# mLSTM cell with mixture of depths: exponents by matrix product, output gates by tanh, state decay on GpSimd, and another order of the layers

## The chip, the cores and the metric

The kernel runs on one core of a Trainium2 chip. The metric is device time in microseconds, from start to end of one execution; the median of several executions counts. A core has a matrix engine (TensorE, "PE" in the profile, with its weight loads as "PEld"), a vector engine (VectorE, "DVE"), a scalar engine for activation functions (ScalarE, "ACT"), a general engine (GpSimd, "POOL"), and a queue engine (SyncE, "SP") which here only issues transfers. Sixteen DMA engines move data between the device memory and the on-chip SBUF; TensorE writes to PSUM, from where VectorE or ScalarE fetch the result.

## What is computed

There are two stages: an mLSTM cell over 4 batches, 8 heads, 768 positions and 40 elements a head, and a mixture of depths over the 4 x 768 tokens of 8 x 40 = 320 elements that it yields.

```python
for t in range(S):                                   # _attn_ref, per batch and head
    m_new  = np.maximum(f_gate[:, :, t] + m, i_gate[:, :, t])
    f_stab = np.exp(f_gate[:, :, t] + m - m_new)
    i_stab = np.exp(i_gate[:, :, t] - m_new)
    m = m_new
    C = f_stab * C + i_stab * einsum('bhd,bhe->bhde', vt, kt)
    n = f_stab * n + i_stab * kt
    h_tilde = einsum('bhde,bhe->bhd', C, qt)
    denom = np.maximum(np.abs(nq), 1.0)              # nq = n . q
    y[:, :, t] = sigmoid(o_gate[:, :, t]) * h_tilde / denom

scores = np.einsum('bsd,d->bs', x, w_gate)           # _moe_ref
out = x.copy()
for b in range(B):
    top_idx = np.argpartition(-scores[b], capacity)[:capacity]      # capacity 128
    xe = x[b, top_idx]
    ye = np.maximum(xe @ w1, 0.0) @ w2                               # 320 -> 1024 -> 320
    out[b, top_idx] = xe + sigmoid(scores[b, top_idx])[:, None] * ye
```

Both kernels compute the first stage in chunks of 128 positions: inside a chunk as a masked matrix of weighted products of keys and queries, between chunks by a state C that decays. There are 6 chunks in a batch and 24 in all.

## The kernel before

The gates are handled for all 32 rows (batch x head) at once. A running sum F of the forget gates and a running maximum Mg of a = i - F are made chunk by chunk. Mg is written to device memory (M_d), so that it can be read back spread over all 128 partitions; a comes as one column for each head.

```python
for c in range(NT):
    nc.vector.tensor_tensor_scan(out=F[:, c, :], ...)                     # L143
    nc.vector.tensor_tensor(out=a[:, c, :], in0=i_sb[:, c, :], in1=F[:, c, :], op=OP.subtract)
    nc.vector.tensor_tensor_scan(out=Mg[:, c, 0:L], ...)                  # L146
    ...
    nc.scalar.dma_start(out=M_d[c], in_=Mg[:, c, :])
    pc = ps_t.tile([128, 3, BH], FP, name="pc", tag="t")
    for j, row in enumerate((a, wk, r)):
        nc.tensor.transpose(pc[:, j, :], row[:, c, :], ident[0:BH, 0:BH]) # L157
    ...
```

Every chunk loads k, q, v and the spread Mb. The weights W = exp(a - M) are made by one activation for each head, with a as its bias; the mask is set beforehand.

```python
def load_chunk(b, c):
    ...
    nc.sync.dma_start(out=Mb, in_=_bcast(M_d[c][b * H:(b + 1) * H, :], 128))

def mlstm_chunk(b, c, qk, v1, Mb, C, so, x, sc):
    nc.gpsimd.affine_select(out=Mb[:, :, 0:L], ..., fill=BIG, ...)        # L177
    for h in range(H):
        nc.scalar.activation(out=W[:, h // 2, h % 2, :], in_=Mb[:, h, 0:L], func=AF.Exp,
                             bias=cols[c][:, 0, ...], scale=-1.0)         # L181
    # ... pt: transposes of k and q (L188), copied to qkT by ScalarE (L189)
    # ... pS = k q (L198), P = pS * W on VectorE (L200)
    # ... pI = C q (L207), num = pI * r (L210)
    # ... wv = v * wk on GpSimd (L215), pC = k wv (L221)
    for j in range(2):
        nc.vector.tensor_tensor(out=Cj, in0=Cj, op=OP.mult, in1=decay...) # L229
        nc.vector.tensor_tensor(out=Cj, in0=Cj, in1=pj, op=OP.add)        # L231
    # ... pH = P v (L236), num = num + pH (L240), den, rec (L243 to L246)
    nc.gpsimd.tensor_tensor(out=sor, in0=so[:, c], in1=rec..., op=OP.mult)         # L248
    nc.vector.tensor_tensor(out=x[:, c, :]..., in0=num[:, :, 0:D], in1=sor, ...)   # L249
    nc.vector.tensor_tensor_reduce(out=scr, in0=x[:, c, :], in1=wg, ..., accum_out=sc[:, c:c + 1])  # L252
    for dst in (x_d[b], out[b]):
        nc.gpsimd.dma_start(out=dst[c * L:(c + 1) * L, :], in_=x[:, c, :])         # L255
```

The output gates of a whole batch are loaded and put through a sigmoid in one piece. `compare` sets the scores of one chunk against those of all chunks so far (pb L262, sb L263, ge L265); `ranks` makes ranks of them (pcol L274, sel); `gather` finds the chosen rows (pidx) and fetches them by an indirect transfer from x_d (L301); `layer1` and `layer2` are the two layers (ph L331, py L342), after which ye is written to its rows in out by an indirect transfer (L345). The layers of a batch come in one piece, in the fifth chunk of the next batch; of the last two batches' layers, all come after the last chunk:

```python
            elif c == NT // 2 + 1 and b < B - 1:
                layer2(b - 1, layer1(b - 1, todo))
    compare(*steps[-1], *state[B - 1][1])
    before_last = layer1(B - 2, todo) if B > 1 else []
    sels = ranks(B - 1, *state[B - 1][1][2:])
    layer2(B - 2, before_last)
    layer2(B - 1, layer1(B - 1, gather(B - 1, sels)))
```

A framework around the kernel sets all waits by which tile is written and read by whom, and puts the instructions of each engine in an order of its own; pools of buffers decide when a tile may be written anew.

Of the kernel before, what the change touches and what calls it, by code (L numbers as in the profile page):

```python
# [9 lines left out]
FP = mybir.dt.float32  # L10
# [17 lines left out]
def kernel(  # L28
# [35 lines left out]
    NB = 4  # L64
    GE = [L * u * (u + 1) // 2 for u in range(NT + 1)]
    HALVES = [slice(0, 64), slice(64, 128)]
    AHEAD = 2

    assert S == NT * L and D < DP and H == 2 * NP and BH <= 128 and F_ == NFC * 128 and 0 < capacity < S <= 2048
# [14 lines left out]
    f_sb = gate.tile([BH, NT, L], FP, name="f_sb")  # L84
    i_sb = gate.tile([BH, NT, L], FP, name="i_sb")
    nc.sync.dma_start(out=f_sb, in_=f_gate.rearrange("b h (c p) -> (b h) c p", p=L))
    nc.sync.dma_start(out=i_sb, in_=i_gate.rearrange("b h (c p) -> (b h) c p", p=L))
# [3 lines left out]
    for n in range(NB):  # L91
        nc.gpsimd.memset(qk_t[n][:, :, :, D:DP], 0.0)
        nc.gpsimd.memset(v_t[n][:, :, D:DP], 1.0)

    def load_chunk(b, c):
        n = (b * NT + c) % NB
        t = slice(c * L, (c + 1) * L)
        for j, src in enumerate((k, q)):
            nc.sync.dma_start(out=qk_t[n][:, j, :, 0:D], in_=src[b, :, t, :].rearrange("h p d -> p h d"))  # L99
        nc.sync.dma_start(out=v_t[n][:, :, 0:D], in_=v[b, :, t, :].rearrange("h p d -> p h d"))  # L100
        Mb = work.tile([128, H, L + 1], FP, name="Mb", bufs=NB)
        nc.sync.dma_start(out=Mb, in_=_bcast(M_d[c][b * H:(b + 1) * H, :], 128))
        return qk_t[n], v_t[n], Mb

    ident = const.tile([128, 128], FP, name="ident")
    make_identity(nc, ident)
    iota_i = const.tile([128, capacity], I32, name="iota_i")
    nc.gpsimd.iota(iota_i, pattern=[[1, capacity]], channel_multiplier=0)
    iota_f = const.tile([128, capacity], FP, name="iota_f")
    nc.vector.tensor_copy(out=iota_f, in_=iota_i)  # L110

    token_i = const.tile([128, NT], I32, name="token_i")
    nc.gpsimd.iota(token_i, pattern=[[L, NT]], channel_multiplier=1)
    token = const.tile([128, NT], HF, name="token")
    nc.vector.tensor_copy(out=token, in_=token_i)
    later = const.tile([128, NT], FP, name="later")
    nc.vector.tensor_scalar(out=later, in0=token_i, scalar1=-1.0, scalar2=float(S - 1), op0=OP.mult, op1=OP.add)
    earlier = const.tile([128, NT * L], BF, name="earlier")
    nc.gpsimd.memset(earlier, 1.0)
    nc.gpsimd.affine_select(out=earlier[:, S - L:], in_=earlier[:, S - L:], compare_op=OP.is_gt, fill=0.0, base=0,  # L120
                            pattern=[[-1, L]], channel_multiplier=1)
    ones_b = const.tile([128, 1], BF, name="ones_b")
    nc.gpsimd.memset(ones_b, 1.0)
    xe_t = [const.tile([128, NDC * 128], FP, name=f"xe{n}") for n in range(2 * len(SLOTS))]
    n_xe = [0]
    for n in range(len(xe_t)):
        nc.gpsimd.memset(xe_t[n], 0.0)
    x_d = [dram.tile([S, DM], FP, name=f"x_d{b}") for b in range(B)]
    ones = const.tile([BH, L], FP, name="ones")
    nc.vector.memset(ones, 1.0)  # L130


    F = gate.tile([BH, NT, L], FP, name="F")
    a = gate.tile([BH, NT, L], FP, name="a")
    Mg = gate.tile([BH, NT, L + 1], FP, name="Mg")
    r = gate.tile([BH, NT, L], FP, name="r")
    wk = gate.tile([BH, NT, L], FP, name="wk")
    m = gate.tile([BH, NT + 1], FP, name="m")
    nM = gate.tile([BH, NT], FP, name="nM")
    nc.vector.memset(m[:, 0:1], -BIG)  # L140
    M_d, cols = [], []
    for c in range(NT):
        nc.vector.tensor_tensor_scan(out=F[:, c, :], data0=ones, data1=f_sb[:, c, :], initial=0.0,  # L143
                                     op0=OP.mult, op1=OP.add)
        nc.vector.tensor_tensor(out=a[:, c, :], in0=i_sb[:, c, :], in1=F[:, c, :], op=OP.subtract)
        nc.vector.tensor_tensor_scan(out=Mg[:, c, 0:L], data0=ones, data1=a[:, c, :], initial=m[:, c:c + 1],  # L146
                                     op0=OP.mult, op1=OP.max)
        nc.vector.tensor_tensor(out=m[:, c + 1:c + 2], in0=F[:, c, L - 1:L], in1=Mg[:, c, L - 1:L], op=OP.add)
        nc.vector.tensor_scalar(out=nM[:, c:c + 1], in0=Mg[:, c, L - 1:L], scalar1=-1.0, scalar2=None, op0=OP.mult)
        nc.scalar.activation(out=r[:, c, :], in_=Mg[:, c, 0:L], func=AF.Exp, bias=m[:, c:c + 1], scale=-1.0)  # L150
        nc.scalar.activation(out=wk[:, c, :], in_=a[:, c, :], func=AF.Exp, bias=nM[:, c:c + 1], scale=1.0)
        nc.vector.tensor_copy(out=Mg[:, c, L:L + 1], in_=r[:, c, L - 1:L])
        M_d.append(dram.tile([BH, L + 1], FP, name=f"M_d{c}"))
        nc.scalar.dma_start(out=M_d[c], in_=Mg[:, c, :])
        pc = ps_t.tile([128, 3, BH], FP, name="pc", tag="t")
        for j, row in enumerate((a, wk, r)):
            nc.tensor.transpose(pc[:, j, :], row[:, c, :], ident[0:BH, 0:BH])  # L157
# [275 lines left out]
```

## Time and profile before

| Quantity | Value |
|---|---|
| Time, median of three executions | 268.16 us (264.06 to 270.69) |
| Profiled execution: span | 261.3 us |
| Mean granted TensorE clock | 0.88 of full speed |
| Bytes moved | 41.07 MB, mean 157 GB/s |
| W, exponents: 192 activations | 61.2 us of ACT, 392 ns each |
| qkT, evictions: 48 copies of 128x512 | 26.9 us of ACT, 581 ns each |
| Table loads on ACT | 11 of 1283 ns |
| C, decay: 32 products of 40x164 | 11.9 us of DVE, 371 ns each |
| ph, first layer: 192 matmul instructions | 27.1 us of PE |
| py, second layer: 64 matmul instructions | 18.0 us of PE |

A line of instructions in the profile gives start, duration, engine, line of the kernel, operation, the tile written and the tiles read, and in brackets how long the engine had been idle before it and what ended that. A line of waits gives who waited for whom, the total in microseconds, the number of waits and the longest. A line of a queue gives packets, megabytes and the share of sixteen engines' span. A stretch gives its bounds and length, then busy time (and number of instructions) of PE, PEld, DVE, ACT and POOL, then the granted clock, the DMA share and GB/s. The DMA line has one digit, in tenths, for each fortieth of the span.

### The profile page before, as it was taken

What the parts mean: (1) busy time and instruction counts of PE and PEld (TensorE: products, weight loads), DVE (VectorE), ACT (ScalarE), POOL (GpSimd) and SP (SyncE); (2) the same over time, 40 slices, a digit from 0 to 9 for tenths busy, and PEclk for the clock granted to TensorE, in tenths of its full rate; (3) what the DMA queues carried; (4) which work ended last, traced back from release to release, by engine and by line L of the source; (5) the groups of instructions that cost most, each with busy time, mean ns of one, the idle gap of its engine ahead of it and who ended that gap; (6) DMA issues with size and microseconds to landing.
All of it is one profiled execution on the core that took longest, in us unless ns stands there. A gap on an engine that the chain in (4) does not pass through costs nothing.

```text
span 261.3 us, 6263 instructions
## 1 busy us (share of the span) xinstructions
PE 189.9 (73%) x2402; PEld 160.6 (61%) x2402; DVE 148.7 (57%) x443; ACT 120.1 (46%) x304; POOL 105.5 (40%) x155
## 2 busy tenths in 40 slices
PE   0498204875987968899799687998969862982980
PEld 0376103764966856887687576976859752961950
DVE  5813303687767998831779799347876985021000
ACT  2484049776568455760556578237633300000000
POOL 8435322635365455643643655443354222003001
PEclk9999855797799988799999979999995995798696
DMA  8979899999799899996599999717533121001000
GB/s 119 147 272 222 288 205 226 224 194 238 163 238 264 198 203 230 238 185 227 102 177 215 221 211 258 222 75 152 130 81 113 41 75 50 3 0 50 3 0 25
DMA packets 107085, 41.07 MB, mean 157 GB/s; under 512 B 101328, under 2 KB 101520, under 8 KB 107056
## 3 DMA queue, kind: packets, MB, share of 16 engines
q1 hardware_dynamic: 103392, 28.61, 55.8%
q0 software_dynamic: 3376, 11.96, 13.6%
q8 instruction: 19, 0.31, 0.5%
q10 hardware_dynamic: 288, 0.10, 0.2%
q14 instruction: 10, 0.08, 0.1%
HBM read 32.05 MB, written 8.62 MB: 156 GB/s over the span
## 4 chain that ended last, share of the span: by engine, by line
issue 23%; DMA 20%; DVE 19%; PE 12%; SPq 10%; POOL 10%; ACT 2%; POOLq 1%; ACTq 0%; DVEq 0%
DMA Mb<-M_d 10%; POOL sor L248 5%; SPq L350 5%; PE pH L236 3%; DVE P L200 3%; DVE x L249 3%; SPq L100 3%; DMA out_dram<-x 3%; PE ph L331 2%; DMA qk<-in_k_dram 2%; SPq L99 2%; DVE ge L265 2%; POOL Mb L177 2%; DMA so<-in_o_gate_dram 2%; DVE C L229 2%
## 5 line engine op out<-in xcount | busy, mean ns | idle before, releaser
L181 ACT ACTIVATE W<-Mb,cols 128x128 f32<-128x128 f32 x192 | 61.2, 392 | 22.8 <-POOL Mb L177 11.8
L236 PE MATMUL pH<-v,P 128*64 128x64 f32 x768 | 30.9, 232 | 24.9 <-DVE P L200 19.7
L236 PEld LDWEIGHTS pH<-v,P 128*64 128x64 f32 x768 | 26.5, 144 | 30.9 <-issue 15.4
L200 DVE TENSOR_TENSOR P<-pS,W 128x512 f32<-128x512 f32 x48 | 31.9, 680 | 17.0 <-ACT W L181 16.6
L177 POOL TENSOR_SCALAR_AFFINE_SELECT Mb<-Mb 128x1024 f32<-128x1024 f32 x24 | 26.9, 1121 | 35.8 <-DMA Mb<-M_d 35.0
L198 PE MATMUL pS<-qkT 64*128 64x128 f32 x384 | 35.6, 319 | 3.0 <-ACT qkT L189 3.0
L188 PE MATMUL pt<-ident,qk 128*128 128x128 f32 x192 | 35.2, 309 | 1.1 <-ACT qkT L189 0.8
L198 PEld LDWEIGHTS pS<-qkT 64*128 64x128 f32 x384 | 29.3, 216 | 7.9 <-ACT qkT L189 4.2
L248 POOL TENSOR_TENSOR sor<-so,rec 128x320 f32<-128x320 f32 x24 | 17.3, 722 | 40.8 <-DVE rec L246 31.7
L189 ACT COPY qkT<-pt 128x512 f32<-128x512 f32 x48 | 26.9, 581 | 14.3 <-PE pt L188 14.2
L331 PE MATMUL ph<-xeT,w 128*128 128x128 f32 x192 | 27.1, 311 | 3.0 <-DVE xeT L323 1.6
L331 PEld LDWEIGHTS ph<-xeT,w 128*128 128x128 f32 x192 | 26.3, 225 | 4.1 <-DVE xeT L323 2.2
L188 PEld LDWEIGHTS pt<-ident,qk 128*128 128x128 f32 x192 | 23.4, 154 | 4.1 <-ACT qkT L189 1.4
L207 PE MATMUL pI<-C,qkT 128*64 128x128 f32 x320 | 25.3, 307 | 0.0
L249 DVE TENSOR_TENSOR x<-num,sor 128x320 f32<-128x320 f32 x20 | 11.4, 570 | 18.9 <-POOL sor L248 18.9
L215 POOL TENSOR_TENSOR wv<-v,cols 128x328 f32<-128x328 f32 x20 | 15.1, 754 | 17.3 <-PE pC L221 6.5
L207 PEld LDWEIGHTS pI<-C,qkT 128*64 128x64 f32 x320 | 20.0, 154 | 2.9 <-issue 0.8
L265 DVE SCALAR_TENSOR_TENSOR ge<-sb,sc,earlier 128x128 bf16<-128x128 f32 (+5 forms) x24 | 19.9, 830 | 2.9 <-ACT sb L263 2.4
L255 POOL DMA_DIRECT2D x_d<-x x24 | 14.1, 590 | 17.7 <-DVE x L249 17.1
L262 PE MATMUL pb<-ident,sc 128*128 128x128 f32 x24 | 8.5, 356 | 15.8 <-DVE sc L252 15.8
L344 DVE SCALAR_TENSOR_TENSOR ye<-py,g,xe 128x320 f32<-128x320 f32 x4 | 2.2, 550 | 30.8 <-PE py L342 30.8
L263 ACT COPY sb<-pb 128x128 f32<-128x128 f32 x24 | 6.2, 260 | 28.5 <-PE pb L262 28.5
(84 smaller groups left out, 250.1 us busy)
## 6 DMA issues: line engine op xcount, KB each, us to landing
Mb<-M_d SPq DMA_DIRECT2D x24, 516.0 KB, 5.6
qk<-in_k_dram SPq DMA_DIRECT2D x24, 160.0 KB, 5.1
qk<-in_q_dram SPq DMA_DIRECT2D x24, 160.0 KB, 5.0
v<-in_v_dram SPq DMA_DIRECT2D x24, 160.0 KB, 4.5
so<-in_o_gate_dram SPq DMA_DIRECT2D x24, 160.0 KB, 4.6
x_d<-x POOLq DMA_DIRECT2D x24, 160.0 KB, 3.2
out_dram<-x POOLq DMA_DIRECT2D x24, 160.0 KB, 3.6
w<-in_moe_w_dram POOLq DMA_DIRECT2D x1, 1280.0 KB, 12.8
```

The source lines that it names most:

```text
L177: nc.gpsimd.affine_select(out=Mb[:, :, 0:L], in_=Mb[:, :, 0:L], compare_op=OP.is_ge, fill=BIG, base=0, pattern=[[0, H], [1, L]], channel_m ...
L181: nc.scalar.activation(out=W[:, h // 2, h % 2, :], in_=Mb[:, h, 0:L], func=AF.Exp, bias=cols[c][:, 0, b * H + h:b * H + h + 1], scale=-1.0)
L188: nc.tensor.transpose(pt[:, p, :], qk[:, j, 2 * p:2 * p + 2, :].rearrange("s a d -> s (a d)"), ident)
L189: nc.scalar.copy(out=qkT[:, j], in_=pt)
L198: nc.tensor.matmul(pS[j][:, p, :], qkT[e, 0, p, :], qkT[e, 1, p, :], start=True, stop=True)
L200: nc.vector.tensor_tensor(out=P[:, :, j, :], in0=pS[j], in1=W[:, :, j, :], op=OP.mult)
L207: nc.tensor.matmul(pI[t, 2 * p:2 * p + 2, :].rearrange("t a d -> t (a d)"), qkT[:, 1, p, t], C[:, p].rearrange("e a d -> e (a d)"), start= ...
L236: nc.tensor.matmul(pH[t, h, :], P[:, h // 2, h % 2, t], v1[:, h, :], start=True, stop=True)
L248: nc.gpsimd.tensor_tensor(out=sor, in0=so[:, c], in1=rec.unsqueeze(2).to_broadcast([128, H, D]), op=OP.mult)
L249: nc.vector.tensor_tensor(out=x[:, c, :].rearrange("p (h d) -> p h d", d=D), in0=num[:, :, 0:D], in1=sor, op=OP.mult)
L265: nc.vector.scalar_tensor_tensor(out=ge[:, GE[u]:GE[u + 1]], in0=sb.rearrange("p t l -> p (t l)")[:, 0:n], scalar=sc[:, u:u + 1], in1=earl ...
L331: nc.tensor.matmul(ph[:, f, :], w1[:, j, (f0 + f) * 128:(f0 + f + 1) * 128], xeT[:, j, :], start=(j == 0), stop=(j == NDC - 1))
```

## The change

The change has seven parts.

1. **Exponents by a product.** Instead of spreading Mg by a transfer through device memory, a - M is made by TensorE. M and a are each split into three bf16 numbers whose sum is the fp32 number, and placed (by a product with a table, `place`) in 32 rows for each group of four heads, beside rows of ones; a bf16 product over these 32 rows then gives a - M of four heads at once, 128x512, in PSUM. One exponent evicts it. The mask comes after that, on W. This removes M_d, Mb and the bias columns. The gates are loaded four times, into four groups of 32 partitions, since the placement reads the parts from there; the scans run over several chunks at once.
2. **Output gates by tanh.** sigmoid(x) = (1 + tanh(x/2)) / 2; tanh and 1 + ... are done on each chunk's gates, which are loaded with the chunk, and the factor 2 goes into the denominator.
3. **Decay on GpSimd.** There are three state buffers; GpSimd writes the decayed state into the next one and VectorE adds the new part.
4. **x stored once.** The gather reads from out instead of from x_d, and the indirect transfers name only the rows up to their own batch.
5. **Layers over three chunks.** First half of layer 1 in the fourth chunk, second half in the fifth, layer 2 in the sixth. For the third batch layer 1 so lies in the last batch.
6. **Ranking first in the tail.** The last batch's ranking and gather come ahead of the third batch's layer 2.
7. **Preparation one chunk ahead.** W, wv, the transposes and the tanh of chunk n + 1 (`prepare`) are written before the rest of chunk n; loads run three chunks ahead with five buffers instead of two with four.

```diff
-    NB = 4
+    NB = 5
-    AHEAD = 2
+    AHEAD = 3
...
+    def load_f_i(c0, c1):
+        for dst, src, eng in ((f_sb, f_gate, nc.sync), (i_sb, i_gate, nc.scalar)):
+            for g in G:
+                eng.dma_start(out=dst[g, c0:c1], in_=src.rearrange("b h (c p) -> (b h) c p", p=L)[:, c0:c1])
...
+    def split(x3, x, g):
+        nc.vector.tensor_copy(out=x3[:, g], in_=x[:, g])
+        nc.vector.tensor_tensor(out=rest[64:128, g], in0=x[64:128, g], in1=x3[64:128, g], op=OP.subtract)
+        nc.vector.tensor_copy(out=x3[64:128, g], in_=rest[64:128, g])
+        nc.vector.tensor_tensor(out=x3[96:128, g], in0=rest[96:128, g], in1=x3[96:128, g], op=OP.subtract)
+        nc.vector.memset(x3[0:BH, g], 1.0)
+
+    def operands(u, c):
+        pX = ps_m.tile([128, 2, L], FP, name="pO", tag="m")
+        for j, x3 in enumerate((M3, a3)):
+            nc.tensor.matmul(pX[:, j, :], place[j][u]..., x3[:, c, :], start=True, stop=True)
+        ...
+        nc.scalar.copy(out=a_o[u, c], in_=pX[:, 1, :])
+        nc.vector.tensor_tensor(out=M_o[u, c], in0=pX[:, 0, :].unsqueeze(1).to_broadcast([128, 4, L]), op=OP.mult,
+                                in1=which.unsqueeze(2).to_broadcast([128, 4, L]))
...
+    def prepare(b, c, qk, v1, so):
+        for h0 in range(0, H, 4):
+            rows_in = slice(64 * (b % 2) + 8 * h0, 64 * (b % 2) + 8 * h0 + 32)
+            pW = ps_t.tile([128, 4, L], FP, name="pW", tag="t")
+            nc.tensor.matmul(pW, a_o[b // 2, c][rows_in], M_o[b // 2, c][rows_in], start=True, stop=True)
+            nc.scalar.activation(out=W[:, h0:h0 + 4, :], in_=pW, func=AF.Exp)
+        nc.gpsimd.affine_select(out=W, in_=W, compare_op=OP.is_ge, fill=0.0, base=0, ...)
+        ...                                    # wv; transposes pt, copied to T
+        nc.scalar.activation(out=so, in_=so, func=AF.Tanh, scale=0.5)
+        nc.scalar.add(so, so, 1.0)
...
-        for h in range(H):
-            nc.scalar.activation(out=W[:, h // 2, h % 2, :], in_=Mb[:, h, 0:L], func=AF.Exp, ...)
...
+                nc.gpsimd.tensor_tensor(out=Cn[:, :, :, 0:D1], in0=C[:, :, :, 0:D1], op=OP.mult, ...)
-                    nc.vector.tensor_tensor(out=Cj, in0=Cj, op=OP.mult, in1=decay...)
...
-        for dst in (x_d[b], out[b]):
-            nc.gpsimd.dma_start(out=dst[c * L:(c + 1) * L, :], in_=x[:, c, :])
+        nc.gpsimd.dma_start(out=out[b, c * L:(c + 1) * L, :], in_=x[:, c, :])
...
+    def rows(b):
+        return out[0:b + 1].rearrange("b s d -> (b s) d")
...
+    load(0)
+    load_f_i(1, NT)
+    gates(0, 1)
+    prepared(0)
+    load(1)
+    gates(1, 3)                                # gates(3, NT) at the second chunk
...
-            elif c == NT // 2 + 1 and b < B - 1:
-                layer2(b - 1, layer1(b - 1, todo))
+            elif c == 3:
+                todo = enter(todo)
+                layer1(todo, 0)
+            elif c == 4:
+                layer1(todo, 1)
+            elif c == 5 and b < B - 1:
+                layer2(b - 1, todo)
     compare(*steps[-1], *state[B - 1][1])
-    before_last = layer1(B - 2, todo) if B > 1 else []
-    sels = ranks(B - 1, *state[B - 1][1][2:])
-    layer2(B - 2, before_last)
-    layer2(B - 1, layer1(B - 1, gather(B - 1, sels)))
+    picked = gather(B - 1, ranks(B - 1, *state[B - 1][1][2:]))
+    if B > 1:
+        layer2(B - 2, todo)
+    picked = enter(picked)
+    for half in range(2):
+        layer1(picked, half)
+    layer2(B - 1, picked)
```

Here the names of the pieces are new where the order asks for it: `gates(c0, c1)` does the scans, maxima, split and operands of the chunks c0 to c1 - 1, and `enter` gathers the gate value and the transposes of the chosen rows that `layer1` did before.

## The prediction

> **What bounds the kernel now.** I read the head of the page first, then the DMA line in 40 slices with the table of queues, then the stretches, the table of waits, and the timeline at both ends.
>
> ```profile
> span 261.3 us, 6263 instructions
> PE 189.9 (73%) x2402; PEld 160.6 (61%) x2402; DVE 148.7 (57%) x443; ACT 120.1 (46%) x304; POOL 105.5 (40%) x155
> DMA  8979899999799899996599999717533121001000
> q1 hardware_dynamic: 103392, 28.61, 55.8%
> q0 software_dynamic: 3376, 11.96, 13.6%
> ```
>
> No engine is full, but the transfers are near full until about 170 us. The loads (q1) carry 28.61 MB: 24 Mb broadcasts of 516 KB (12.7 MB) and 96 loads of 160 KB. Next the stretches; the columns are PE, PEld, DVE, ACT and POOL busy, the granted clock, the DMA share and GB/s:
>
> ```profile
> 30.00:40.00 10.00, 0.00 (x0) 0.00 (x0) 0.00 (x0) 3.73 (x3) 3.92 (x6) 0.56 1.04 198
> 40.00:75.00 35.00, 26.42 (x378) 22.66 (x380) 24.30 (x64) 26.35 (x73) 15.76 (x22) 0.78 1.04 211
> 110.00:145.00 35.00, 31.91 (x433) 26.71 (x432) 21.61 (x59) 17.67 (x51) 15.52 (x22) 1.00 0.83 186
> 180.00:218.00 38.00, 29.75 (x485) 25.39 (x483) 30.07 (x93) 14.02 (x40) 14.26 (x22) 0.88 0.33 90
> 0.00:218.00 218.00, 162.61 (x2240) 137.24 (x2240) 142.78 (x426) 117.28 (x298) 101.33 (x150) 0.90 0.83 184
> ```
>
> There are three regimes. Up to 75 us the transfers bind, with ten microseconds in which PE does nothing. From 110 us PE is the fullest engine (31.91 of 35). At the end of the body the DMA share is 0.33 and yet PE has 8 us idle of 38: there DVE (30.07) and its exchange with POOL set the pace. The waits name the two causes:
>
> ```profile
> POOL Mb L177 <- DMA Mb<-M_d: 35.0, 18, 4.9
> POOL sor L248 <- DVE rec L246: 31.7, 14, 4.3
> DVE x L249 <- POOL sor L248: 22.4, 24, 2.2
> ```
>
> The score instructions (scr, one for each chunk) serve as milestones: the first two and the last from the DVE timeline.
>
> ```profile
> 26.07 0.49 DVE L252 CUSTOM_DVE_ANT_0 scr<-x,wg 128x320 f32<-128x320 f32 x1
> 48.73 0.49 DVE L252 CUSTOM_DVE_ANT_0 scr<-x,wg 128x320 f32<-128x320 f32 x1
> ...
> 218.23 0.49 DVE L252 CUSTOM_DVE_ANT_0 scr<-x,wg 128x320 f32<-128x320 f32 x1
> ```
>
> Chunk 5, the last of batch 0, has its scr at 79.92. So the span divides into 80 us for batch 0, 138 us for the other 18 chunks, 36 us for the tail up to the last scatter (issued at 254.45), and 7 us of landing and end. The tail, from the timeline:
>
> ```profile
> 221.30 7.76 PE L331 MATMUL ph<-xeT,w 128*128 128x128 f32 x48 [1.34 <-DVE rank L277]
> 228.90 0.67 PE L274 MATMUL pcol<-ones_b,ge 128*128 128x1 bf16 x21
> 229.82 4.57 PE L342 MATMUL py<-w,hT 128*128 128x320 f32 x16 [0.25 <-DVE rank L278]
> 236.59 1.07 POOL L301 DMA_INDIRECT xe<-x_d,idx  x1 [0.30 <-issue]
> 241.22 8.05 PE L331 MATMUL ph<-xeT,w 128*128 128x128 f32 x48 [0.65 <-DVE xeT L323]
> ```
>
> The ranking of the last batch, on which everything after depends, stands behind the third batch's first layer (7.76 us), and its 1x128 index product behind that batch's second layer.
>
> [...]11 table loads of 1283 ns, 14.1 us of ACT. [...]six o_gate loads (960 KB) take 7.63 us to issue under backlog, 126 GB/s. [...]wv (128x328) takes 754 ns there and num (128x328) 489 on DVE, 1.54 times. [...]no 512-column bf16 product is in this trace.
>
> **The change part by part.**
>
> *Transfers.* Out go 24 Mb broadcasts (12.7 MB) and 24 stores to x_d (3.9 MB); the gates are loaded four times instead of once (+0.6 MB). 41 MB become about 25. But the 98304 packets of 160 B stay. Estimate for a chunk: 640 KB at 126 GB/s is 5.2 us, a store 0.5 us (q0's 13.6% of 261.3 us for 11.96 MB): 5.7 us, with 9 us once for the weights. That is under what PE needs below, so DMA leaves the path; the 35 us wait on Mb goes.
>
> *ACT.* Eight exponents of 392 ns a chunk become two evictions of 512 columns (as qkT's, 581 ns): 3.1 to 1.2 us. Tanh and the addition on 320 elements are perhaps 0.45 us each, for 0.3 us of sigmoid. Ten table loads go. About 120 falls to 95 us; ACT was not the bound.
>
> *PE.* Before 218 us it was busy 162.6 us. From that I take two complete passes of the layers, 13.0 us each (ph 6.8, py 4.5, pX 0.7, pcol 0.7, pidx 0.3: a quarter of each group), 1.0 for the third ranking and 5.3 for the pc transposes: 130 / 24 = 5.4 us a chunk. Each chunk gains two 512-column products, 0.45 us, and each chunk of the first two batches a pair of small placement products.
>
> *DVE.* A chunk costs about 5.2 us (148.7 less 10.3 of gate work and 13 of layers, over 24). The decay product L229 (11.9 us in 20 chunks, 0.6 each) goes to GpSimd, leaving 4.6. Against it the gate work grows: the three-part split is four operations of 768 elements for M and as many for a, some 9 us, and M_o is six 128x512 products from PSUM at 680 ns. With scans (4.8), the four elementwise passes (5), cols (1.4) and the placement tables (4) I make it 29 us in batch 0 instead of 10, and 4 us more in batch 1. The order of instructions has these pieces between P, num and x of the first chunks, not ahead of them.
>
> *POOL.* Decay in (about 0.75 us), one store issue out (0.57): no change in load, near 3.9 us a chunk.
>
> *Batch 0.* DVE needs 29 + 6 x 4.6 = 57 us from the gates' arrival at about 4.5: chunk 5 at 62 instead of 80. PE (6 x 5.9 and the placements from about 10 us, so to 46) and DMA (6 x 5.7 from 3, so to 37) are below that. First scr at 22 to 25, as before; the second at about 36 instead of 49. Gain 18.
>
> *The other 18 chunks.* PE was busy about 115 of these 138 us. Add the third batch's first layer from the tail (7.5), 18 x 0.45 = 8 and 1 for placements: 132. PE's gaps behind a late Mb go, and the layers' halves over chunks 3, 4 and 5 give PE filling work. I choose 90% full, as in 110:145: 147 us. So this part gets 9 us longer and the last scr is at 209.
>
> *The tail.* From the last scr: compare 2.5, pcol with its wait 0.9, rank 0.2, sel 1.0, pidx and idx 0.8, gather 3.0 (236.59 to 239.58), g and xeT 1.6, ph and py 12.4, ye to scatter 0.9: 23.3. The third batch's py (4.6) now lies beside the gather, and outlasts it by about 1: 24.3 instead of 36.2. Gain 12.
>
> *Sum.* 209 + 24.3 + 6.9 = 240 us of span, 21 less. Another piece is in that 90%: the scatter formerly addressed the whole of out and so waited for later stores (4.96 us for out_dram<-x before the scatter at 173.81); rows(b) ends that. The three timed runs have their median 5 us above the profiled execution (268.16 to 263.01), with few stalls on DMA perhaps 4: I predict 244.
>
> **The rivals.** *PE merely replaces DMA as bound:* if PE stays as full as in 80:218 before (83.5%), 132 us of work take 158, and the time is about 255. For it: at 180:218, without DMA pressure, PE was only 78% full; DVE's bubble at x stays, and POOL gets another 0.75 us ahead of sor. Against: DVE drops by 0.6 us a chunk and P often fills that bubble. *ACT blocks the in-order queue:* pW and pt now share two PSUM buffers, four evictions a chunk, and the tanh waits for the load issued last of its chunk; when it is late, W and T behind it are late. That would show as PE waiting for ACT and give 250 to 258; 3.6 us of ACT work in a 6 to 8 us period speaks against. *The gate prologue is worse:* if M, a and the split come strictly before the chunks, batch 0 takes 75, and the time 257. *The clock:* it was 0.90 up to 218; with fewer gaps at 0.97 PE's work is 8 us less, and the time 232.
>
> **Range and chances.** Two of the rivals together would give 262 to 266, within 2% of 268; a faster clock with full PE gives 230. Range 231 to 259. Faster by over 2% (below 262.8) 0.92, within 2% 0.05, slower 0.03, the last if both the prologue and ACT's queue go badly.
>
> **What would show it.** Chunk 5's scr near 62 and the last near 209; no wait on Mb; DMA share below 0.8 in the body; one table load; PE near 90% from 80 us on and first in the chain; the last scatter some 24 us after the last scr. It would be wrong if sor or W became the longest waits, if chunk 5 came after 72, or if PE's groups ph and py cost more when cut into pieces.

## The result and the profile after

| Quantity | Before | After |
|---|---|---|
| Time, median of four executions | 266.77 us (264.06 to 270.69) | 252.0 us (249.98 to 257.17) |
| Ratio after to before, with 95% interval | | 0.9499 (0.941 to 0.9589) |
| Span of the profiled execution | 261.3 us | 250.0 us |
| Start of scr in chunk 0, 1, 5 | 26.1, 48.7, 79.9 us | 30.1, 55.2, 80.3 us |
| Start of the last scr | 218.2 us | 222.0 us |
| Last scatter issued | 254.45 us | 245.09 us |

Executions of one kernel fall into a faster and a slower group, and a ratio with an interval compares the faster ones alone, so it can differ from the quotient of the medians.

The change makes the kernel 5% faster (3% when it was measured again, experiment 3), as the prediction had it in kind: 244 us was said, with 231 to 259 as range. But the 11.3 us that the span lost do not lie where they were looked for. The stretch from the last score to the last scatter went from 36.2 to 23.1 us, a gain of 13.1; what follows it went from 6.85 to 4.9, a gain of 1.9; everything ahead of it became 3.8 us *longer*. Batch 0, which was to give 18 us, gave nothing.

First the head of the page, two lines of its 40 slices, and the two lines of queues that answer to those shown of before.

```profile
span 250.0 us, 6255 instructions
...
PE 202.1 (81%) x2474; PEld 162.7 (65%) x2474; DVE 166.1 (66%) x450; ACT 89.9 (36%) x199; POOL 110.4 (44%) x148
...
PEclk9998555579999999889999999999999999995998
DMA  4999999539864766573346666563250110000000
...
q1 hardware_dynamic: 100224, 16.13, 42.4%
q0 software_dynamic: 2224, 8.03, 10.0%
```

The transfers are relieved as foreseen: after the seventh slice only one digit of DMA is a 9, and q1 carries 16.13 instead of 28.61 MB. PE, the fullest engine before too, is now busy for 81% instead of 73%. The line to stop at is PEclk: five tenths in slices 5 to 8, that is from 25 to 50 us, and again near the end.

The stretches; columns as in the prediction (PE, PEld, DVE, ACT and POOL busy, granted clock, DMA share, GB/s).

```profile
20.00:30.00 10.00, 3.95 (x44) 2.52 (x44) 9.34 (x23) 2.85 (x9) 6.27 (x8) 0.63 1.30 220
30.00:40.00 10.00, 9.34 (x48) 6.71 (x50) 8.03 (x18) 6.47 (x13) 3.72 (x4) 0.50 1.09 234
40.00:50.00 10.00, 10.00 (x87) 8.01 (x83) 4.69 (x10) 2.40 (x8) 2.22 (x3) 0.50 0.71 90
50.00:60.00 10.00, 9.90 (x126) 8.19 (x127) 7.54 (x23) 5.61 (x13) 5.75 (x8) 0.83 0.61 109
...
80.00:222.00 142.00, 127.14 (x1766) 104.89 (x1766) 101.46 (x275) 55.83 (x124) 68.51 (x81) 0.99 0.44 88
110.00:140.00 30.00, 29.66 (x396) 23.95 (x394) 18.52 (x50) 12.43 (x29) 12.45 (x16) 1.00 0.53 103
```

Read the first three from left to right. From 20 to 30 us DVE is full (9.34) and PE is mostly waiting (3.95). From 30 to 50 us PE is full, yet it finishes few instructions: 48 and 87, where the next ten microseconds hold 126. It is full because its clock is at 0.50. From 80 us on PE is busy 127.14 of 142 us, and 29.66 of 30 in the middle: there it is the bound.

That slices 5 to 8 were not the first slow ones is told by the durations of one group, eight transposes of k or q (pt):

```profile
15.28 1.97 PE L233 MATMUL pt<-ident,qk 128*128 128x128 f32 x8
...
34.40 1.97 PE L233 MATMUL pt<-ident,qk 128*128 128x128 f32 x8
```

At 70.1 us the same group takes 1.09 us. So PE was at half speed at 15 us already, where the record of the clock still says 1.00 (from 15 to 17 us).

The waits. No line on Mb is left; the exchange of sor between DVE and POOL is what it was before.

```profile
POOL sor L302 <- DVE rec L300: 31.9, 16, 5.6
...
DVE x L303 <- POOL sor L302: 22.3, 23, 1.6
...
ACT so L236 <- DMA so<-in_o_gate_dram: 10.5, 7, 4.8
...
DVE M_o L168 <- ACT a_o L167: 9.3, 3, 3.3
```

The last two are new. They are small, but both have their longest instance in the first microseconds, on the way to the first W.

The milestones again (chunks 0, 1, 5 and the last) and then the tail, from the timelines of DVE, PE and POOL; behind each, the line of before that the prediction does not show.

```profile
30.15 0.48 DVE L306 CUSTOM_DVE_ANT_0 scr<-x,wg 128x320 f32<-128x320 f32 x1
...
55.22 0.63 DVE L306 CUSTOM_DVE_ANT_0 scr<-x,wg 128x320 f32<-128x320 f32 x1
...
80.28 0.49 DVE L306 CUSTOM_DVE_ANT_0 scr<-x,wg 128x320 f32<-128x320 f32 x1
...
222.00 0.49 DVE L306 CUSTOM_DVE_ANT_0 scr<-x,wg 128x320 f32<-128x320 f32 x1
```

```profile
79.92 0.48 DVE L252 CUSTOM_DVE_ANT_0 scr<-x,wg 128x320 f32<-128x320 f32 x1
```

```profile
224.37 0.72 PE L327 MATMUL pcol<-ones_b,ge 128*128 128x1 bf16 x21 [1.42 <-DVE ge L318]
226.33 0.32 PE L347 MATMUL pidx<-token,sel 128*128 128x1 f16 x6 [1.25 <-DVE sel L337]
226.51 6.67 PE L394 MATMUL py<-w,hT 128*128 128x320 f32 x16
...
227.12 1.05 POOL L353 DMA_INDIRECT xe<-out_dram,idx  x1 [4.28 <-DVE idx L349]
...
234.28 5.62 PE L386 MATMUL ph<-xeT,w 128*128 128x128 f32 x48 [0.78 <-DVE xeT L375]
239.75 4.47 PE L394 MATMUL py<-w,hT 128*128 128x320 f32 x16
...
245.09 1.00 POOL L397 DMA_INDIRECT out_dram<-ye,idx  x1 [10.01 <-DVE ye L396]
```

```profile
254.45 1.01 POOL L345 DMA_INDIRECT out_dram<-ye,idx  x1 [16.79 <-DVE ye L344]
```

The ranking now follows the last score at once, and the third batch's py runs while the gather is under way. That py takes 6.67 us, the same group at the end 4.47.

### The profile page after: what moved, and what is told of

It is laid out like the page before. It is cut to its first block, busy times and chain, and to the rows that moved or that the text cites. A ratio compares the mean times of both kernels' runs of the same rounds, so it can differ in the third digit from the quotient of the medians.

```text
span 250.0 us, 6255 instructions
## 1 busy us (share of the span) xinstructions
PE 202.1 (81%) x2474; PEld 162.7 (65%) x2474; DVE 166.1 (66%) x450; ACT 89.9 (36%) x199; POOL 110.4 (44%) x148
## 2 busy tenths in 40 slices
DMA packets 102860, 24.94 MB, mean 100 GB/s; under 512 B 100688, under 2 KB 100944, under 8 KB 102832
## 3 DMA queue, kind: packets, MB, share of 16 engines
q1 hardware_dynamic: 100224, 16.13, 42.4%
## 5 line engine op out<-in xcount | busy, mean ns | idle before, releaser
L250 PE MATMUL pS<-T 64*128 64x128 f32 x384 | 40.6, 311 | 0.1
L250 PEld LDWEIGHTS pS<-T 64*128 64x128 f32 x384 | 31.5, 202 | 9.4 <-issue 7.2
L221 ACT ACTIVATE W<-pW 128x512 f32<-128x512 f32 x48 | 26.9, 596 | 24.8 <-PE pW L220 24.5
L222 POOL TENSOR_SCALAR_AFFINE_SELECT W<-W 128x1024 f32<-128x1024 f32 x24 | 28.2, 1175 | 17.1 <-ACT W L221 16.9
L289 PEld LDWEIGHTS pH<-v,P 128*64 128x64 f32 x768 | 27.0, 145 | 12.4 <-DVE num L264 6.1
L302 POOL TENSOR_TENSOR sor<-so,rec 128x320 f32<-128x320 f32 x24 | 17.6, 731 | 32.0 <-DVE rec L300 31.9
L234 ACT COPY T<-pt 128x512 f32<-128x512 f32 x48 | 26.6, 587 | 11.7 <-PE pt L233 11.5
L261 PE MATMUL pI<-C,T 128*64 128x128 f32 x320 | 24.3, 290 | 0.0
L316 ACT COPY sb<-pb 128x128 f32<-128x128 f32 x24 | 6.4, 266 | 45.9 <-PE pb L315 45.9
L308 POOL DMA_DIRECT2D out_dram<-x x24 | 14.1, 589 | 18.1 <-DVE x L303 16.5
L275 POOL TENSOR_TENSOR C<-C,cols 128x328 f32<-128x328 f32 x16 | 16.1, 1008 | 12.5 <-DVE C L284 10.4
L394 PE MATMUL py<-w,hT 128*128 128x320 f32 x64 | 20.6, 475 | 0.0
L261 PEld LDWEIGHTS pI<-C,T 128*64 128x64 f32 x320 | 18.6, 142 | 2.9 <-issue 0.6
```

What stands on the lines that cost most here:

```text
L221: nc.scalar.activation(out=W[:, h0:h0 + 4, :], in_=pW, func=AF.Exp)
L222: nc.gpsimd.affine_select(out=W, in_=W, compare_op=OP.is_ge, fill=0.0, base=0, pattern=[[0, H], [1, L]], channel_multiplier=-1)
L234: nc.scalar.copy(out=T[:, j], in_=pt)
L250: nc.tensor.matmul(pS[j][:, p, :], T[e, 0, p, :], T[e, 1, p, :], start=True, stop=True)
L261: nc.tensor.matmul(pI[t, 2 * p:2 * p + 2, :].rearrange("t a d -> t (a d)"), T[:, 1, p, t], C[:, p].rearrange("e a d -> e (a d)"), start=Tr ...
L289: nc.tensor.matmul(pH[t, h, :], P[:, h // 2, h % 2, t], v1[:, h, :], start=True, stop=True)
```

## The experiments

Each is compared with the kernel before on the same chip. The letters in the expectations name theories as the expectations put them; in short, A is PE working slowly after a pause in batch 0, B the gate work on DVE, C the memsets on GpSimd, P PE as bound of the body, T the tail as the place of the gain, R the other parts as gaining too; L and D are rivals of P. "Milestones" are the starts of scr in chunks 0, 1, 5 and the last.

**1. The tail alone.** The kernel before with parts 5 and 6 only: layers over three chunks, ranking first.

```diff
-            elif c == NT // 2 + 1 and b < B - 1:
-                layer2(b - 1, layer1(b - 1, todo))
+            elif c == 3:
+                todo = enter(todo)
+                layer1(todo, 0)
+            ...                                  # and the tail of the changed kernel
```

> The kernel before with parts 5 and 6 alone (layers over three chunks, ranking first in the tail). Theory T (the tail made the whole gain): the body takes the third batch's first layer, 7.5 us of PE work, into gaps it had anyway, last scr at 219 to 223, last scatter 23 to 24 us after it; span 247 to 252, ratio 0.94 to 0.96, as the whole change. Rival R (the other parts gain too): the body grows by the full 7.5 us and the scatter still waits for later stores of out; span 255 to 259, ratio 0.97 to 0.985.

Measured: 257.45 us, ratio 0.9758 (0.9553 to 0.9963). Milestones 28.5, 47.6, 79.6 and 224.2, last scatter at 248.19. The last score comes 6 us later than before, since the third batch's first layer has moved ahead of it, and the tail takes 24.0 us. Rival R's figures came, not T's: these two parts gain 2.4% by themselves (the interval leaves 0.4 to 4.5%), where the whole change gained 5.0 and, on the same chip as here, 3.3%.

**2. All but the tail.** The changed kernel with the order of layers and tail of the kernel before.

```diff
-            elif c == 3:
-                todo = enter(todo)
-                layer1(todo, 0)
-            ...
+            elif c == NT // 2 + 1 and b < B - 1:
+                layer2(b - 1, layer1(b - 1, todo))
```

> The changed kernel with the layers in one piece in the fifth chunk and the old order of the tail. Theory T: nothing is left of the gain but the 7.5 us of PE work that leaves a full PE: chunk 5 at 80, last scr at 213 to 217, tail 34 to 36, span 253 to 260, ratio 0.96 to 0.985. Rival R: the other parts gain by themselves, span under 250, ratio under 0.95. If the other parts cost more than they bring, ratio 1.0 or above.

Measured: 262.98 us, ratio 0.9886 (0.9826 to 0.9947). Parts 1 to 4 and 7 together, with 16 MB fewer transfers and ten table loads fewer, are worth 1.1%: slightly less than theory T gave them, and far from R. So the tail makes most of the gain. The product of the two ratios, 0.965, agrees with the 0.9675 of the next experiment, on the same chip, but lies outside the interval of the first measurement of the whole change (0.941 to 0.9589); the two intervals are wide enough that nothing follows on what the parts do together.

**3. The changed kernel again**, unchanged, as a measure of how far two measurements on two chips differ.

> The changed kernel once more, for the spread and for the granted clock of batch 0. Theory A (the half clock from 25 to 53 us cost about 10 us): an execution whose clock is not halved there has chunk 1's scr at about 46 instead of 55 and ends 6 to 10 us earlier, unless something later takes it. Rival B (the gate work on DVE sets batch 0): chunk 1's scr stays at 52 to 56 whatever the clock. Ratio 0.94 to 0.96.

Measured: 255.54 us, ratio 0.9675 (0.9543 to 0.9808); milestones 31.6, 56.7, 81.8, 225.9. Batch 0 has the same shape, 25 us between the first two scores in both. Its clock line differs from that of the first profile, though; one line of the page and two of the PE timeline:

```profile
PEclk9999999999999999889999999999999968975998
```

```profile
35.86 1.97 PE L233 MATMUL pt<-ident,qk 128*128 128x128 f32 x8
...
71.64 1.09 PE L233 MATMUL pt<-ident,qk 128*128 128x128 f32 x8
```

The record says nine tenths or more at 36 us, and the same eight products take 1.97 us there and 1.09 us later. So the record of the granted clock missed the slow stretch in this run; durations of equal groups show it in both.

**4. and 5. Keeping PE busy in the prologue.** If the pause makes PE slow, useless products in the pause should keep it fast. The first has 50 of 512 columns, in two blocks; the second 56, tied to the pieces of gate work so that they fall between them.

```diff
+    def warm(n):
+        pZ = ps_m.tile([128, 512], FP, name="pZ", tag="m")
+        for _ in range(n):
+            nc.tensor.matmul(pZ, again[:, 0, :], flat(again)[:, 0:512], start=True, stop=True)
...
+    warm(18)
     gates(0, 1)
...
+    warm(32)
     gates(1, 3)
```

> The changed kernel with 50 products without use (bf16, 512 columns, of a constant) on PE, 18 before the first gates and 32 between the first chunk's transposes and the second piece of gates, so that PE is not idle from 3 to 25 us. Theory A: the clock stays at 1.0 from 10 us on, chunk 1's scr at 44 to 48, chunk 5's at 68 to 73, span 240 to 245. Rival B: the clock rises but chunk 1 stays at 52 to 56 and the span at 248 to 253.

> The changed kernel with 56 bf16 products of 512 columns without use, tied to the pieces of the gate work (18 before, 10 behind the first gates, 20 within the second piece's split, 8 at chunk 1), so that PE has no long pause between 3 and 34 us. Theory A (PE works at half speed until 54 us, as the durations of its instructions show, 1.97 us for eight pt instead of 1.10, because it was idle before): pt at full speed (110 to 120 ns each) for chunks 1 and 2, chunk 1's scr at 43 to 47, chunk 5's at 70 to 73, span 6 to 9 us under the changed kernel's. Rival B (the gate work on DVE sets chunk 1): pt is fast, but chunk 1 stays at 51 or later, and the span within 3 us.

Measured: 252.98 us, ratio 0.9545 (0.9352 to 0.9737), milestones 35.1, 52.7, 78.5, 223.6; and 260.45 us, 0.9794 (0.9416 to 1.0173), milestones 37.4, 53.9, 81.5, 229.8. Theory A's figures came in neither; the first falls on rival B's. The products do raise PE's speed where they stand: in the first, the last 24 ran from 16.7 to 22.8 us, and two small transposes (pc) at 23.7 us took 0.28 us. But behind four short pauses, 1.4 us together, the same two took 0.40 us at 29.1 us, and the pt group at 30.7 us 1.97 us. In the second the pt group at 14.3 us took 1.15 us, so it was fast; but behind a pause of 3.98 us four of the useless products took 1.87 us at 21.2 us (24 took 6.11 in the first), the next pt group at 37 us was slow again, and the first chunk came 6 to 7 us later. They shorten the way from chunk 0 to chunk 1 (17.6 and 16.5 us instead of 25.1), at the price of a later chunk 0. In both, half speed came back after the products or between them; whether PE can be kept at full speed through the whole prologue these two don't settle.

**6. Half of the gate work.** M and a as one bf16 number each: the second and third parts stay zero, and three of the split's five operations are left out, with what they contribute to the exponents; a fourth, the ones, is done once, on GpSimd.

```diff
-        nc.vector.tensor_copy(out=x3[:, g], in_=x[:, g])
-        nc.vector.tensor_tensor(out=rest[64:128, g], in0=x[64:128, g], in1=x3[64:128, g], op=OP.subtract)
-        ...
+        nc.vector.tensor_copy(out=x3[32:64, g], in_=x[32:64, g])
```

> The changed kernel with M and a as one bf16 number each instead of three (the second and third parts are zero): the subtractions, second and third roundings of the split are left out, some 9 us of DVE work in batch 0. Theory A: PE is still slow and full from 30 us on; chunk 1 comes only as much earlier as PE can start on it, 2 to 5 us, at 50 to 53. Rival B: chunk 1's scr at 44 to 48 and chunk 5's at 71 to 74.

Measured: 247.91 us, ratio 0.9326 (0.9112 to 0.954); milestones 31.1, 42.8, 71.2, 215.8. Its stretches, in the same columns:

```profile
20.00:30.00 10.00, 9.33 (x76) 7.04 (x75) 8.81 (x18) 6.25 (x15) 6.99 (x9) 1.00 1.20 192
30.00:40.00 10.00, 9.54 (x133) 7.82 (x132) 8.70 (x20) 5.22 (x13) 5.78 (x8) 1.00 1.13 230
```

Chunk 1 is 12 us earlier and chunk 5 nine, and PE gets 133 instructions done from 30 to 40 us instead of 48. The first product of chunk 1 that needs the gate work is pW, first in the changed kernel and then here, with two pt groups behind it:

```profile
28.90 0.60 PE L220 MATMUL pW<-M_o,a_o 32*128 32x512 bf16 x1
```

```profile
21.85 0.61 PE L220 MATMUL pW<-M_o,a_o 32*128 32x512 bf16 x2
...
23.27 1.97 PE L233 MATMUL pt<-ident,qk 128*128 128x128 f32 x8
...
27.98 0.99 PE L233 MATMUL pt<-ident,qk 128*128 128x128 f32 x7
```

pW starts 7 of the 12 us earlier. This decides for B: the gate work on DVE is what the beginning of chunk 1 waits for. The other 5 us come behind pW, and there A is not refuted: PE is at half speed here too at 23 us, beside a recorded clock of 1.00, but back at full speed from 28 us on, while the changed kernel gets there at about 53 us (nine pI took 1.33 us at 39.6 and 0.76 us at 53.3). Why it gets there so much earlier the run does not show.

**7. GpSimd's constants first.** The memsets and index tables that GpSimd makes stand ahead of the first gates instead of behind them.

```diff
+    # constants, masks, memsets of xe: moved up to here
     load_f_i(1, NT)
     gates(0, 1)
```

> The changed kernel with the memsets of the constants and states ahead of the first gates, while POOL waits for the first v. Theory C (POOL's memsets at 12 to 20 us slow DVE: iota_f 0.82 us against 0.20 in the kernel before): DVE's work between 12 and 30 us shrinks by 3 to 5 us, chunk 0's scr at 26 to 28 instead of 30 to 32, chunk 1 as much earlier. If C is wrong, they stay within 1 us, or the slowing moves into the first gates.

Measured: 251.69 us, ratio 0.9524 (0.9346 to 0.9701); milestones 30.4, 51.6, 76.0, 220.2. The first chunk is not earlier, which was missed; chunks 1 and 5 are 4 us earlier, and the time is not measurably another. What the memsets do is seen in the changed kernel's DVE and POOL timelines:

```profile
13.49 0.73 POOL L446 MEMSET earlier<- 128x768 bf16 x1
...
13.87 0.82 DVE L437 CAST iota_f<-iota_i 128x128 f32<-128x128 int32 x1
14.01 0.70 DVE L442 CAST token<-token_i 128x6 f16<-128x6 int32 x1
...
14.08 0.63 DVE L444 TENSOR_SCALAR later<-token_i 128x6 f32<-128x6 int32 x1
...
14.20 0.41 POOL L454 MEMSET xe<- 128x384 f32 x1
```

Three small DVE instructions begin 0.14 and 0.07 us apart and all end at 14.69 to 14.71, right after GpSimd's memset ends at 14.61. With the memsets out of the way they take 0.22, 0.17 and 0.17 us. But this is not where the 4 us come from. Chunk 1's first pW starts at 29.14 us, 0.2 us later than in the changed kernel; what differs is PE's speed behind it. The same nine products, in the changed kernel and here:

```profile
39.60 1.33 PE L261 MATMUL pI<-C,T 128*64 128x128 f32 x9
```

```profile
39.56 0.76 PE L261 MATMUL pI<-C,T 128*64 128x128 f32 x9
```

PE is back at full speed some 14 us earlier than in the changed kernel. Experiment 9, which leaves the memsets where they were, has that too, so this experiment does not show what the memsets cost in chunk 1.

**8. The new product twice.** Each pW product is issued twice, the second overwriting the first: 48 more 512-column products.

```diff
             nc.tensor.matmul(pW, a_o[b // 2, c][rows_in], M_o[b // 2, c][rows_in], start=True, stop=True)
+            nc.tensor.matmul(pW, a_o[b // 2, c][rows_in], M_o[b // 2, c][rows_in], start=True, stop=True)
```

> The changed kernel with each pW product done twice: 48 more bf16 products of 512 columns, 0.43 us a chunk at full speed. Theory P (in the last 18 chunks PE is the bound): last scr 7 to 9 us later, the span 8 to 11 us longer. Rival L (the exchange between DVE, POOL and ACT sets the period, PE has room): under 4 us longer.

Measured: 263.74 us (259.72 to 264.84), beside 266.39 us of the kernel before, a ratio of 0.990 for which there is no interval. The profiled execution has a span of 258.0 us, 8.0 and 3.5 us above the two of the changed kernel. The eighteen chunks after batch 0 took 146.7 us (83.8 to 230.5), where the changed kernel took 141.7 and 144.2: 2.5 to 5 us of the whole. In batch 0, chunk 5 came 2 to 3.5 us later. The 36 more products in the eighteen chunks would be some 8 us, an estimate from experiment 5, where ten useless products of 512 columns took 2.32 us (at 10.1 us) and five took 1.25 us (at 24.9 us), 214 ns for each one more. So a third to two thirds of the added work lengthened the stretch, and PE's share of it rose from 90 to 92%. This lies between P and rival L: PE is the bound for part of the stretch, and the rest of the added work went into its gaps.

**9. Decay back on DVE.** Part 3 undone, with the state buffers left as they are.

```diff
-                nc.gpsimd.tensor_tensor(out=Cn[:, :, :, 0:D1], in0=C[:, :, :, 0:D1], op=OP.mult, ...)
+                nc.vector.tensor_tensor(out=Cn[:, :, :, 0:D1], in0=C[:, :, :, 0:D1], op=OP.mult, ...)
```

> The changed kernel with the decayed state written by DVE instead of GpSimd (16 products of 128x328, about 0.49 us each). Theory P (PE is the bound of the last 18 chunks, DVE has room[...]): within 1% of the changed kernel, the scr of 1.49 us are gone. Rival D (DVE is the bound there): 6 to 8 us longer.

Measured: 251.0 us, ratio 0.9396 (0.9304 to 0.9488); milestones 29.9, 52.1, 77.4, 221.2. The interval overlaps that of the changed kernel: moving the decay to GpSimd brings nothing that can be measured. The product takes 1008 ns on GpSimd and 710 ns here. Rival D, DVE as bound of the last 18 chunks, is out: they took 143.8 us. The slow scr that were to be gone are still there: 2.53, 2.57 and 1.50 us in three chunks. Chunks 1 and 5 come 3 to 5 us earlier than in the changed kernel, though gates, memsets and the tanh are the same, and here too PE was fast early; sixteen pC:

```profile
38.68 0.77 PE L272 MATMUL pC<-wv,qk 128*64 128x41 f32 x16
```

In the changed kernel the same sixteen took 1.45 us (40.51 to 41.96 us), with one pI among them.

**10. Gate work on ScalarE.** Experiment 7, and besides: the two roundings of the split, and the four products that make M_o, as ScalarE activations; the memset of ones on GpSimd; the first chunk's tanh bound behind M_o. Nothing is left out.

```diff
-        nc.vector.tensor_copy(out=x3[:, g], in_=x[:, g])
+        nc.scalar.copy(out=x3[:, g], in_=x[:, g])
...
-        nc.vector.tensor_tensor(out=M_o[u, c], in0=pX[:, 0, :]..., op=OP.mult, in1=which...)
+        for h in range(4):
+            nc.scalar.activation(out=M_o[u, c][:, h, :], in_=pX[:, 0, :], func=AF.Copy, scale=which[:, h:h + 1])
```

> The changed kernel with the work ahead of the chunks taken off DVE and the same results: roundings of the split and M_o on ScalarE, ones by GpSimd, constants of GpSimd ahead of the first gates, the first chunk's tanh bound behind M_o. Some 9 us of DVE work in batch 0 go, and 3 us of waiting for the first output gates. Theory B: chunk 0's scr at 25 to 28, chunk 1's at 40 to 45, chunk 5's at 67 to 72, span 240 to 246, ratio 0.91 to 0.935. If PE's half speed rather than DVE's work sets batch 0, chunk 1 stays above 48.

Measured: 245.7 us (245.47 to 246.45), ratio 0.92 (0.9124 to 0.9277), which is clear of the changed kernel's 0.941 to 0.9589. Milestones 32.6, 48.3, 73.9, 216.4: chunk 0 comes 1 to 3 us later, the others 6 to 10 earlier, which is less than expected, and chunk 1 lies above 48, the sign that the expectation named for PE's half speed. A stretch of it shows it:

```profile
30.00:40.00 10.00, 10.00 (x50) 6.65 (x50) 3.90 (x8) 6.95 (x21) 4.28 (x5) 1.00 1.10 228
```

DVE has come free (3.90), and PE is full with 50 instructions, so still at half speed: four pt took 1.11 us at 33.6 us, and eight 1.15 us at 45.9. The clock record says 1.00 here too. Which of the changes put together here made the gain is not separated.

**11. Only the tanh later.** The first chunk's tanh gets its bias from an instruction that reads M_o, so that ScalarE can't take it up before the first operands.

```diff
+            nc.scalar.activation(out=none, in_=M_o[0, 0][:, 0, 0:1], func=AF.Copy, scale=0.0)
+            nc.scalar.activation(out=so, in_=so, func=AF.Tanh, bias=none, scale=0.5)
```

> The changed kernel with the first chunk's tanh bound behind M_o (its bias is a zero made from M_o), so that ScalarE does not wait for the first output gates before it evicts a_o. Theory: the 3.3 us that M_o waits go and chunk 0's scr comes 2 to 3 us earlier; chunk 1 0 to 3 us earlier, since the second piece of gates follows on DVE at once; the time within 1% of the changed kernel.

Measured: 249.39 us (245.9 to 253.81) beside 266.56 us, a ratio of 0.936 without interval; milestones 29.3, 50.2, 75.6, 218.5. Chunk 0 is 1 to 2 us earlier, as the theory had it or somewhat less. Chunks 1 and 5 are 5 us earlier, more than the 3.3 us of wait that was taken away; but chunk 1's pW starts only 0.8 us earlier (28.06), and behind it PE is fast early, as in experiments 7 and 9 (nine pI in 0.76 us at 38.0). So 1 to 2 us are shown for the wait, and not 5. What was in the way stands in the changed kernel's timeline:

```profile
12.11 0.47 ACT L236 ACTIVATE so<-so 128x320 f32<-128x320 f32 x1 [4.79 <-DMA so<-in_o_gate_dram]
...
12.99 0.25 ACT L167 CAST a_o<-pO 128x128 bf16<-128x128 f32 x1
...
13.27 0.69 DVE L168 TENSOR_TENSOR M_o<-pO,which 128x512 bf16<-128x512 f32 x1 [3.32 <-ACT a_o L167]
```

ScalarE sits 4.79 us before a tanh whose gates have not landed, the cast of the first operands stands behind it in the queue, and DVE loses 3.32 us to that. In this experiment the cast starts at 9.38 us.

**12. Keeping PE busy in the tail.** Experiment 10 with 36 useless products in PE's three pauses between the last pH and the third batch's py.

```diff
+    keep(22, ge_z[...], flat(again)[:, 0:256])
+    keep(6, sb_z[:, NT - 1, :], ident)
     sels = ranks(B - 1, *state[B - 1][1][2:])
+    keep(8, ge_z[...], flat(again)[:, 0:256])
```

> The version with the gate work taken off DVE, and in the tail 36 products without use on PE (22 before the last compare, 6 behind its score row, 8 behind the ranking's products), which fill PE's pauses of 3.3, 1.4 and 1.3 us there. Theory A in its small form (a PE that pauses for a few microseconds works at half speed for some time): py of the third batch takes 4.5 us instead of the 6.7 of the changed kernel, and the span is 1.5 to 2.5 us shorter than without. If the pauses have nothing to do with it, py stays at 6 or more and the span the same or 1 us longer.

Measured: 244.27 us (243.77 to 246.19), ratio 0.9183 (0.9113 to 0.9252); last score at 215.6, last scatter at 237.0. The same group in PE's timeline, first in experiment 10 and then here:

```profile
220.88 6.79 PE L399 MATMUL py<-w,hT 128*128 128x320 f32 x16
```

```profile
220.46 4.55 PE L399 MATMUL py<-w,hT 128*128 128x320 f32 x16
```

With the pauses filled, py takes 4.55 instead of 6.79 us, and the tail 21.4 instead of 23.2. So the pauses of 3.3, 1.4 and 1.3 us cost the py behind them 2.2 us. The gain in time is within the two intervals.

## Why the prediction was right, and where it was wrong

*The tail* was right in its reason and its size: 24.3 us predicted, 23.1 measured. Inside it two terms were off and cancelled: py outlasts the gather by 3 us rather than 1 (6.67 us after PE's pause, where the prediction had 4.6), and the last batch's two layers took 10.1 us, not 12.4. Experiment 1 puts this part in the kernel before and finds the same 24.0.

*The other 18 chunks* were right in kind: 147 us predicted, 141.7 measured, so the stretch grew by 3.4 us and not by 9. PE was 90% busy as chosen (127.14 of 142), with 127 us of work where the sum had 132 (it began with 115 us of before; the trace has 116.6; its 0.45 us a chunk for the two new products was an estimate, and the 214 ns of experiment 8 make it 0.43), at a mean clock of 0.99 where it was 0.93 before. That PE takes the place of the transfers as bound, the first rival in a milder form, rests on the 29.66 of 30 us in the middle, on a DMA share that fell from 0.72 to 0.44, and on experiments 8 (in part) and 9 (it is not DVE). This would be why 16 MB less of transfers bring so little: they left the path and uncovered PE at nearly the same height.

*Transfers, ACT and the decay.* 41.07 MB became 24.94 (25 said), ACT 120.1 us became 89.9 (95 said). The table loads of 1283 ns went from 11 to one, as estimated; tanh and the addition take 0.47 us each, where 0.45 was said. The decay product takes 1.0 us on GpSimd, not the 0.75 that wv (754 ns on GpSimd) led to, and moving it has no measurable effect; DVE's 0.6 us a chunk were not on the path.

*Batch 0* is the step that failed. "DVE needs 29 + 6 x 4.6 = 57 us from the gates' arrival at about 4.5: chunk 5 at 62 instead of 80." The amount of work was right: up to 80 us DVE was busy 59.3 us. What failed is the assumption that DVE would be busy all along, for which I relied on the order of instructions, and on the line that PE's work would be done "to 46". At the first score 5 to 8 us were lost (predicted at 22 to 25, measured at 30), at the second 19 (36 and 55); from the second to the sixth score the forecast of 26 us stands against 25.1 measured. What the runs show in place of that step:

- *Late operands.* The second and third piece of gate work take DVE from 14 to 42 us, with P, num and x between them as the order said; but from 20 to 30 us PE has little to do until the operands of the next chunk come out of them. An order on DVE that keeps DVE busy is no help to an engine that waits for the last item of the list. Without the split's operations chunk 1 begins 7 us earlier and ends 12 us earlier (experiment 6). This is the third rival, the prologue, which I gave too little.
- *PE at half speed,* a term the sum had not at all. From 30 to 50 us PE was busy 19.3 us at a clock of 0.50; at full speed that would be about 10 us of work, an estimate from these two numbers. By the durations of equal groups it was back at full speed at about 53 and 55 us in the two profiles of the changed kernel, with the second score at 55.2 and 56.7, and at 37 to 39 us in experiments 7, 9 and 11, with the second score at 50 to 52. Since experiment 9 touched neither the memsets nor the tanh, the 4 and 5 us of experiments 7 and 11 at chunk 1 are no measure of what was changed in these. How the loss divides between late operands and half speed is not separated.
- *A blocked queue.* The tanh for the first chunk held ScalarE while its gates were loading: 1 to 2 us at the first score (experiment 11). This is the second rival, at one single place.
- *Memsets on GpSimd* beside DVE's first gate work: seen in three small instructions, but with no gain at the first score or at chunk 1's pW (experiment 7).

"The clock" stood among the rivals only as a gain. What the runs show of a loss is this. Slow groups stand behind the pause of 3.98 us in experiment 5 (four useless products in 1.87 us; four took 1.02 us at 10.1 us in experiment 4) and behind the tail's pauses of 3.3, 1.4 and 1.3 us in experiment 10 (py in 6.79 us; 4.55 us with the pauses filled in experiment 12); in experiment 4 short pauses of 1.4 us together came before half speed. Being busy did not bring full speed back soon: from 30 to 50 us PE was busy 9.34 and 10.00 of two times ten microseconds and stayed at half. Why it took so long stays open, and so does why it took 14 us less in some runs; experiments 4 and 5 could not settle it.

That the time came within the range although batch 0 missed by 18 us is in part luck: the 18 chunks came out 5 us shorter than forecast, and tail and end together 3, so that the span missed by 10 (250.0 where the sum had 240).

Of the prediction's own signs, no wait on Mb, one table load, the DMA share, PE near 90% and the tail came true; chunk 5 after 72 is the sign it named for being wrong. sor is the longest wait left of the three that it shows, but no longer than before. ph and py did not cost more in pieces (44.4 us together, 45.1 before).

Experiment 10 is what these findings make of the kernel: 8% under the kernel before, where the change had 5 and 3%.

## What to carry to other kernels

When preparation is moved from transfers onto an engine, ask not how much work that engine has, but when the first item that the bounding engine needs comes out of it; work that is needed early belongs on the engine that is idle early. Where a queue is worked off in order, as ScalarE's was here (a cast stood behind a tanh that waited 4.79 us), an instruction that waits for a late load must not stand ahead of one that starts the pipeline (here 1 to 2 us). And judge the matrix engine's speed from the durations of equal groups, early and late: busy time alone hides half speed (9.34 and 10.00 of ten microseconds at a clock of 0.50), and the clock record missed it in experiments 3, 6 and 10. A milestone that moves is no proof that the change moved it, as long as the same groups run at another speed.

## What the runs showed of the hardware that was not expected

- A full PE stayed at half speed for about 20 us: eight pt products took 1.97 us at 34.4 us and 1.09 us at 70.1 us in the changed kernel. Such slow groups stand beside a recorded clock of 1.00 in experiments 6 (eight pt in 1.97 us at 23.3 us) and 10 (four pt in 1.11 us at 33.6 us), and of nine tenths or more in experiment 3 (eight pt in 1.97 us at 35.9 us). How long it lasts differs between profiles with the same prologue: to about 53 us here, to about 38 us in experiment 9.
- A group behind pauses of a few microseconds was slow: py took 6.79 us behind pauses of 3.3, 1.4 and 1.3 us, and 4.55 us when these were filled with useless products.
- DVE instructions took longer beside GpSimd's: iota_f 0.82 us beside memsets, 0.22 with these moved away (experiment 7). scr, usually 0.49 us, took about 1.5 us in three chunks of the changed kernel, each time when GpSimd's wv product began 0.38 to 0.42 us after it, and 2.5 us in experiments 6 and 9 when a second GpSimd instruction followed wv there. But other scr with the same neighbour kept their 0.48 us (at 60.9 and 87.0 us), and one with two instructions in a row took 1.49 (at 94.3 us), so what decides it is open. No experiment took wv away from scr.
